# First chunk's outputs from wide products, and the first pair's sums of squares on TensorE

## The chip, the cores and the metric

The kernel runs on one core of one Trainium2 chip. The metric is the device time of one execution in microseconds (us). Before the change it is 990.29 us, the median of three runs (990.25 to 992.25). All times below that belong to a trace come from one profiled execution, which took 989.57 us.

## What is computed

Attention with random features over 4 batches, 8 heads, 576 positions, 64 values a head and 128 features, then two gated layers on its output:

```python
def phi(x):
    proj = np.einsum('bhsd,md->bhsm', x, omega)
    sq = np.sum(x * x, axis=-1, keepdims=True) / 2.0
    h = proj - sq
    h = h - np.max(h, axis=-1, keepdims=True)
    return np.exp(h) / np.sqrt(m)
q_p, k_p = (phi(q_s), phi(k_s))
kv = np.einsum('bhsm,bhsd->bhmd', k_p, v)
z = np.sum(k_p, axis=2)
num = np.einsum('bhsm,bhmd->bhsd', q_p, kv)
den = np.einsum('bhsm,bhm->bhs', q_p, z)[..., None] + 1e-06
x = num / den                                # 2304 tokens x 512
x = (silu(x @ w_gate) * (x @ w_val)) @ w_out   # 512 -> 1536 -> 512
x = (x @ w_a * (x @ w_b)) @ w_out2
```

All inputs are float32 (q_s and k_s are q and k, scaled).

## The kernel before

The 2304 tokens are cut into five chunks that end at 512, 1024, 1280, 1792 and 2304. The heads go in four pairs, two heads of 64 values to the 128 partitions. Everything that the kernel does is recorded in a plan first: each operation with its engine, an assumed cost, a due time and the tiles that it reads and writes. A list scheduler then fixes one order for each engine. `KEPT` is a tuple of seeds that shift the due times a little, so another tuple gives another order of all operations, not only of those that the diff touches. Every engine takes its list strictly in that order, and SP's list is the order of the loads.

For a pair of heads of the first batch, `keys` loads k twice, d-major (`xT`, 64 values of two heads on 128 partitions by tokens) and token-major (`kt`), and v (`vt`). `features` makes the projections (L642, into ps_m or ps_p, `bd` holds omega), the sums of squares (the token-major tile is squared by ScalarE, L579, in place, and reduced by VectorE, L583, into `s`), the biases (maximum by L653, then L656 and L660) and the exponentials on ScalarE (L666, into `kf`). TensorE sums kf with v (L702, ps_kv), ScalarE copies these sums to `kvs` (L708 the products with v, L712 the sums of the features themselves). For q of the first chunk `queries` does the same into `qf`, and `own` makes the outputs: TensorE transposes qf (L815), ScalarE copies the result to `fT` (L818), TensorE multiplies it with kvs in pieces of 128 tokens by 65 columns a head (L835), VectorE adds 1e-6 to the denominators (L852), takes the reciprocal (L856) and multiplies (L860, into `xt`), and TensorE transposes xt back to d-major (L869). `put` then splits the outputs in a high part `xh` (ScalarE, L780) and a low part `xl` (VectorE, L496) for the products of the layers in fp32r.

`layer` makes each product of a layer as a triple: xh by wh (L1011), xl by wh (L1012), xh by wl (L1013). The weights' parts come from work spread over ScalarE and VectorE: L974 and L971 on ScalarE, L977 (w64a, w64b) and L980 (w) on VectorE, then wh (ScalarE, L992) and wl (VectorE, L496). `a` (L1031, ScalarE, after a load of a table for the function) and `h` (L1039 and L1043, VectorE) are the layer's gate. At the end of the first chunk's attention nine triples with the other three pairs' xh and xl run first; then come the last pair's three, and from there on the triples follow each other. The last two chunks later go through a scheme of seven products for eight (L1080). The first 14 products (L548) multiply an identity only to keep TensorE going while inputs land.

## Time and profile before

| | |
|---|---|
| median of three runs | 990.29 us |
| the profiled execution, its own time | 989.57 us |
| its span on the core | 987.8 us |
| TensorE, products | 977.5 us busy (99%) |
| TensorE, weight loads beside them | 822.6 us (83%) |
| VectorE | 895.1 us (91%) |
| ScalarE | 714.1 us (72%) |
| GpSimd | 266.1 us (27%) |
| granted TensorE clock | full in all 40 slices |

1.8 us of the execution lie around the span. The shares are averages over the whole span; the front, in which attention is made, and the long stretch of the layers behind it have different limits, so the profile is best read by stretches of time. Busy time of TensorE counts modelled ends of overlapping products. In the rows below, a "row" of TensorE is one pass; a float32 product is two of them, a transpose one, a product of fp32r one.

### The profile page before, as it was taken

Reading aid. Unit: us, or ns where it says so; the run is one execution under the profiler, and the core shown is the slowest. Engines: PE = TensorE matmul, PEld = TensorE weight load, DVE = VectorE, ACT = ScalarE, POOL = GpSimd, SP = SyncE. Lnnn points to the kernel's source line nnn. Section 1 sums busy time; section 2 is a strip of 40 time slices with the busy share of each in tenths; the row PEclk is TensorE's granted clock in tenths of the full one; section 3 lists DMA queues with packets and bytes.
Section 4 is the critical chain, followed back from the end, with each engine's and each line's share of the span. In section 5 each row is a group of like instructions: output and inputs, shape, how many; then the busy total and the mean of one; then the engine's idle time right before and its main releaser. Section 6 shows DMA issues by size and latency. Waiting matters only on the chain. (4 is left out here: it accounts for less than half of the span.)

```text
span 987.8 us, 15428 instructions
## 1 busy us (share of the span) xinstructions
PE 977.5 (99%) x5166; PEld 822.6 (83%) x5166; DVE 895.1 (91%) x1629; ACT 714.1 (72%) x1515; POOL 266.1 (27%) x209
## 2 busy tenths in 40 slices
PE   9999999999999999999999999999999999999998
PEld 7878888888888888888789999988888888888886
DVE  6899999999978899999979989888899889989997
ACT  5987888798889997888868877676573645556351
POOL 2310023413403233364457524112020021202020
PEclk9999999999999999999999999999999999999999
DMA  8687876686876657666654465511212301121212
GB/s 279 198 272 227 242 260 188 222 241 207 270 225 199 191 175 235 207 192 218 198 188 119 141 189 164 177 57 33 74 43 64 92 26 53 33 75 44 64 33 86
DMA packets 92544, 153.12 MB, mean 155 GB/s; under 512 B 8752, under 2 KB 41392, under 8 KB 92464
## 3 DMA queue, kind: packets, MB, share of 16 engines
q1 hardware_dynamic: 92384, 152.11, 49.6%
q8 instruction: 40, 0.66, 0.3%
q14 instruction: 40, 0.33, 0.1%
q10 hardware_dynamic: 80, 0.03, 0.0%
HBM read 128.52 MB, written 23.59 MB: 154 GB/s over the span
## 5 line engine op out<-in xcount | busy, mean ns | idle before, releaser
L496 DVE TENSOR_TENSOR wl<-w,wh 128x512 fp32r<-128x512 f32 x254 | 187.3, 747 | 11.5 <-ACT wh L992 11.1
L1011 PE MATMUL ps_m<-xh,wh 128*128 128x512 f32 (+1 forms) x504 | 189.2, 375 | 1.4 <-ACT xh L780 0.7
L1012 PE MATMUL ps_m<-xl,wh 128*128 128x512 f32 (+1 forms) x504 | 184.0, 365 | 0.2 <-DVE xl L496 0.2
L1013 PE MATMUL ps_m<-xh,wl 128*128 128x512 f32 (+1 forms) x504 | 183.8, 365 | 0.0
L992 ACT ACTIVATE wh<-w 128x512 fp32r<-128x512 f32 x220 | 136.9, 633 | 34.9 <-DVE w L980 19.4
L496 POOL TENSOR_TENSOR rs<-xT,rs 64x576 fp32r<-64x576 f32 (+4 forms) x48 | 69.3, 1443 | 225.1 <-ACT rs L599 105.7
L1011 PEld LDWEIGHTS ps_m<-xh,wh 128*128 128x128 f32 x504 | 95.2, 189 | 16.3 <-issue 1.7
L1013 PEld LDWEIGHTS ps_m<-xh,wl 128*128 128x128 f32 x504 | 95.1, 189 | 15.8
L1012 PEld LDWEIGHTS ps_m<-xl,wh 128*128 128x128 f32 x504 | 95.3, 189 | 12.8 <-DVE xl L496 0.5
L1011 PE MATMUL ps_m<-hh,wh 128*128 128x512 f32 (+1 forms) x252 | 94.5, 375 | 0.0
L1012 PE MATMUL ps_m<-hl,wh 128*128 128x512 f32 (+1 forms) x252 | 92.0, 365 | 0.0
L1013 PE MATMUL ps_m<-hh,wl 128*128 128x512 f32 (+1 forms) x252 | 91.9, 365 | 0.0
L977 DVE SCALAR_TENSOR_TENSOR w64a<-w64a 128x512 uint32<-128x512 uint32 x90 | 68.3, 762 | 4.1 <-ACT w64a L974 3.7
L980 DVE SCALAR_TENSOR_TENSOR w<-w,w64a 128x512 uint32<-128x512 uint32 x90 | 65.4, 729 | 3.7 <-ACT w L971 3.6
L974 ACT ACTIVATE w64a<-w64a 128x512 uint32<-128x512 uint32 x90 | 60.9, 684 | 3.2 <-DMA w64a<-w 3.1
L971 ACT ACTIVATE w<-w64a 128x512 f32<-128x512 f32 x90 | 60.6, 677 | 0.1
L1011 PEld LDWEIGHTS ps_m<-hh,wh 128*128 128x128 f32 x252 | 47.6, 189 | 8.5 <-issue 2.0
L1013 PEld LDWEIGHTS ps_m<-hh,wl 128*128 128x128 f32 x252 | 47.6, 189 | 7.9
L1012 PEld LDWEIGHTS ps_m<-hl,wh 128*128 128x128 f32 x252 | 47.7, 189 | 6.2
L1046 ACT ACTIVATE hh<-h 128x512 fp32r<-128x512 f32 (+1 forms) x72 | 40.2, 560 | 17.0 <-DVE h L1043 15.0
L496 DVE TENSOR_TENSOR hl<-h,hh 128x512 fp32r<-128x512 f32 (+1 forms) x72 | 49.2, 685 | 0.7 <-ACT hh L1046 0.3
L900 POOL TENSOR_TENSOR xt<-qf,fT 128x512 f32<-128x512 f32 (+2 forms) x31 | 35.4, 1145 | 49.2 <-ACT qf L666 23.0
(842 smaller groups left out, 2630.5 us busy)
## 6 DMA issues: line engine op xcount, KB each, us to landing
w64a<-w SPq DMA_DIRECT2D x90, 512.0 KB, 4.2
w<-kept SPq DMA_DIRECT2D x180, 256.0 KB, 2.7
kept<-w SPq DMA_DIRECT2D x72, 256.0 KB, 4.8
w64b<-w SPq DMA_DIRECT2D x18, 512.0 KB, 4.7
kt<-k_t SPq DMA_DIRECT2D x16, 320.0 KB, 3.7
vt<-v_t SPq DMA_DIRECT2D x16, 320.0 KB, 4.3
xT<-kT SPq DMA_DIRECT2D x15, 288.0 KB, 3.9
qt<-q_t SPq DMA_DIRECT2D x16, 256.0 KB, 3.6
```

What stands on the lines that cost most here:

```text
L496: eng.tensor_tensor(out=out, in0=a, in1=hi.bitcast(F32), op=ALU.subtract)
L900: nc.gpsimd.tensor_tensor(out=pr.tile.rearrange("p (t h m) -> p t h m", t=2, h=2)[lo_:hi_, i:i + m], in0=f.tile[lo_:hi_, g + i:g + i + m], ...
L971: on(ACT, act(CW + 50), due - ahead - 10, lambda: nc.scalar.activation(out=w.tile, in_=raw.tile[:, :, 1].bitcast(F32), func=AF.Abs, scale= ...
L974: on(ACT, act(CW + 50), due - ahead - 10, lambda: nc.scalar.activation(out=raw.tile[:, :, 0], in_=raw.tile[:, :, 0], func=AF.Copy, scale=0 ...
L977: on(DVE, dve(CW, True), due - ahead - 9, lambda: nc.vector.scalar_tensor_tensor(out=raw.tile[:, :, 0], in0=raw.tile[:, :, 1], scalar=0x80 ...
L980: on(DVE, dve(CW, True), due - ahead - 9, lambda: nc.vector.scalar_tensor_tensor(out=w.tile.bitcast(U32), in0=w.tile.bitcast(U32), scalar= ...
L992: on(ACT, act(CW), due - ahead - 7, lambda: nc.scalar.activation(out=hi.tile.rearrange("p a c -> p (a c)"), in_=w.tile, func=AF.Copy), rea ...
L1011: nc.tensor.matmul(o, lhsT=hi.tile[:, wi], rhs=a, start=first, stop=False)
L1012: nc.tensor.matmul(o, lhsT=hi.tile[:, wi], rhs=b, start=False, stop=False)
L1013: nc.tensor.matmul(o, lhsT=lo.tile[:, wi], rhs=a, start=False, stop=last)
L1046: on(ACT, act(n), due + 2, lambda h=h, hh=hh: nc.scalar.activation(out=hh.tile[:, 0:n], in_=h.tile[:, 0:n], func=AF.Copy), reads=[(h,)], w ...
```

## The change

Three things change.

- `own`: for each of the four pairs the first chunk's outputs come from two calls of two products each, over all 512 tokens at once with 64 result rows a head. One call has the sums of features, repeated over 64 columns, as weights and gives the denominators for each of the 64 values; the other has kvs and gives the numerators. Both land d-major in PSUM. VectorE transposes the denominators in 32 x 32 blocks, adds 1e-6 on one value of each block's row (16 a partition), takes the reciprocal of these 16, transposes them back, repeated, and multiplies the numerators in place. The transposes back on TensorE are gone, and `put` reads the product.
- `features`, for the first pair (`SQUARES = 1`) of the first batch and chunk: the token-major tiles of k and q are not loaded. ScalarE squares the d-major tile, TensorE sums over the partitions with `head` (128 x 2, ones for the rows of a head) in products of 128 tokens by 2 columns, and VectorE copies the 10 and 8 results to `s`.
- `KEPT` holds nine other seeds, so the order of all lists changes.

```diff
     KEPT = (
-        100000, 100002, 100011, 100017, 100041, 100092, 100155, 100377, 100485, 100539,
-        100593, 100638, 100683,
+        100001, 100002, 100007, 100107, 100134, 100242, 100288, 100611, 100936,
     )
...
+    head = fixed("head", [P, 2])
...
+    r_few = ring("few", 1, [P, 2, NT // 32])
...
+    SQUARES = 1
...
+        for h in range(2):
+            for i in range(2):
+                on(DVE, dve(2), -1e6, lambda h=h, i=i: nc.vector.memset(
+                    head.tile[h * D:(h + 1) * D, i:i + 1], float(h == i)), writes=[(head, (h, i))])
...
+        if squares:
+            def of_tok():
+                return tok.tile.rearrange("p t c -> p (t c)")[:, 0:width]
+            on(ACT, act(width), due - 4, lambda: nc.scalar.activation(
+                out=of_tok(), in_=rT.tile[:, 0:width], func=AF.Square),
+                reads=[(rT, *rT.state)], writes=[(tok,)])
+            total = ps_t.buf()
+
+            def add_up():
+                for t in range(nt):
+                    nc.tensor.matmul(total.tile[:, 2 * t:2 * t + 2],
+                                     lhsT=of_tok()[:, step * t:step * t + P], rhs=head.tile,
+                                     start=True, stop=True)
+            on(PE, pe(0.16 * nt), due - 2, add_up, reads=[(tok,), (head, *head.state)],
+               writes=[(total,)])
+            on(DVE, dve(2 * nt), due - 2, lambda: nc.vector.tensor_copy(
+                s.tile[:, 0:nt].rearrange("p t h -> p (t h)"), total.tile[:, 0:2 * nt]),
+                reads=[(total,)], writes=[(s,)])
+        else:
...
-        on(SP, dma(320), due - 8, lambda: nc.sync.dma_start(out=tok.tile, in_=bass.AP(
+        squares = b == 0 and p < SQUARES
+        squares or on(SP, dma(320), due - 8, lambda: nc.sync.dma_start(out=tok.tile, in_=bass.AP(
...
-        fT, xt = r_fT.buf(), r_xt.buf()
+        kv = sums[t0 // S, p]
+        fT = r_fT.buf()
...
-                        on(PE, pe(0.233), d, lambda ps=ps, g=g, i=i, h=h, b=b, col=col:
-                           nc.tensor.matmul(
-                               ps.tile[:, col + VA * h:col + VA * (h + 1)],
-                               lhsT=fT.tile[:, h, P * (g + i):P * (g + i + 1)],
-                               rhs=sums[b, p].tile[:, h], start=True, stop=True,
-                               skip_group_check=True),
...
+        den, num, rec = ps_t.buf(), ps_t.buf(), r_ft.buf()
+
+        def times(ps, weights):
+            def run():
+                for h in range(2):
+                    nc.tensor.matmul(ps.tile[h * D:(h + 1) * D, 0:n], lhsT=weights(h),
+                                     rhs=fT.tile[:, h, 0:n], start=True, stop=True)
+            return run
+        on(PE, pe(0.52), d, times(den, lambda h: kv.tile[:, h, D:VA].to_broadcast([P, D])),
+           reads=[(kv, 1), (fT, *fT.state)], writes=[(den,)])
+        on(PE, pe(0.52), d + 0.1, times(num, lambda h: kv.tile[:, h, 0:D]),
+           reads=[(kv, 0), (fT, *fT.state)], writes=[(num,)])
+        few = r_few.buf()
+        on(DVE, dve(n), d, lambda: nc.vector.transpose(out=rec.tile[:, 0:n], in_=den.tile[:, 0:n]),
+           reads=[(den,)], writes=[(rec,)])
+        on(DVE, dve(n // 32, True), d, lambda: nc.vector.tensor_scalar(
+            out=few.tile[:, 0], in0=rec.tile.rearrange("p (b j) -> p b j", j=32)[:, :, 0],
+            scalar1=eps, scalar2=None, op0=ALU.add), reads=[(rec,)], writes=[(few,)])
+        on(DVE, dve(8 * n // 32), d, lambda: nc.vector.reciprocal(out=few.tile[:, 1], in_=few.tile[:, 0]),
+           writes=[(few,)])
+        on(DVE, dve(n), d, lambda: nc.vector.transpose(
+            out=rec.tile[:, 0:n], in_=few.tile[:, 1].unsqueeze(2).to_broadcast([P, n // 32, 32])),
+           reads=[(few,)], writes=[(rec,)])
+        on(DVE, dve(n), d, lambda: nc.vector.tensor_tensor(
+            out=num.tile[:, 0:n], in0=num.tile[:, 0:n], in1=rec.tile[:, 0:n], op=ALU.mult),
+            reads=[(rec,)], writes=[(num,)])
+        put(1, c, p, num, n, due + length)
```

Three places in the order of the engines' lists follow; a number behind a name is its buffer, and the last is its place in the program's list of tiles. In the changed kernel the projections are L667, the sums of squares L592, the products of the outputs L857, the exponentials L691, fT L847, xh L806, w64a L982, w L985, wl and xl L497, wh L997, kvs L734 and L738, the squaring L585.

TensorE at the start, before:

```order
L548 MATMUL ps_t0_66<-ident0_70 128x128 x7
L642 MATMUL ps_m0_61<-bd0_71,xT0_75 128x256 x2
L642 MATMUL ps_m1_62<-bd0_71,xT0_75 128x256 x2
L642 MATMUL ps_m2_63<-bd0_71,xT0_75 128x256
L642 MATMUL ps_p0_64<-bd0_71,xT1_76 128x256 x2
L642 MATMUL ps_p1_65<-bd0_71,xT1_76 128x256 x2
L642 MATMUL ps_m0_61<-bd0_71,xT2_77 128x256
```

and now:

```order
L554 MATMUL ps_t0_66<-ident0_70 128x128 x7
L667 MATMUL ps_p0_64<-bd0_71,xT1_76 128x256 x2
L667 MATMUL ps_p1_65<-bd0_71,xT1_76 128x256
L667 MATMUL ps_m0_61<-bd0_71,xT0_75 128x256
L592 MATMUL ps_t1_67<-head0_89,kt0_81 128x2 x5
L667 MATMUL ps_m0_61<-bd0_71,xT0_75 128x256
L592 MATMUL ps_t0_66<-head0_89,qt0_108 128x2 x4
L667 MATMUL ps_m1_62<-bd0_71,xT0_75 128x256 x2
L667 MATMUL ps_p1_65<-bd0_71,xT1_76 128x256
```

The projections of q (from xT1) come ahead of those of the keys (from xT0), and the two groups of sums of squares stand among the projections.

VectorE at the last pair's outputs, before:

```order
L852 TENSOR_SCALAR den0_99<-ps_t1_67 128x4
L856 RECIPROCAL rec0_102<-den0_99 128x4
L977 SCALAR_TENSOR_TENSOR w64a_1_161<-w64a_1_161 128x512
L860 TENSOR_TENSOR xt0_114<-ps_t1_67,rec0_102 128x256
L852 TENSOR_SCALAR den1_100<-ps_t0_66 128x4
L496 TENSOR_TENSOR wl4_179<-w320_164,wh4_172 128x512
L856 RECIPROCAL rec1_103<-den1_100 128x4
L860 TENSOR_TENSOR xt0_114<-ps_t0_66,rec1_103 128x256
L977 SCALAR_TENSOR_TENSOR w64a_2_162<-w64a_2_162 128x512
L980 SCALAR_TENSOR_TENSOR w321_165<-w321_165,w64a_1_161 128x512
L496 TENSOR_TENSOR xl3_126<-ps_t1_67,xh3_118 128x512
```

and now:

```order
L865 STREAM_TRANSPOSE ft0_113<-ps_t1_67 128x512
L982 SCALAR_TENSOR_TENSOR w64a_1_163<-w64a_1_163 128x512
L867 TENSOR_SCALAR few0_103<-ft0_113 128x16
L497 TENSOR_TENSOR wl3_180<-w323_169,wh3_173 128x512
L870 RECIPROCAL few0_103<-few0_103 128x16
L985 SCALAR_TENSOR_TENSOR w320_166<-w320_166,w64a_0_162 128x512
L872 STREAM_TRANSPOSE ft0_113<-few0_103 128x512
L985 SCALAR_TENSOR_TENSOR w321_167<-w321_167,w64a_1_163 128x512
L875 TENSOR_TENSOR ps_t0_66<-ps_t0_66,ft0_113 128x512
L497 TENSOR_TENSOR wl4_181<-w320_166,wh4_174 128x512
L982 SCALAR_TENSOR_TENSOR w64a_2_164<-w64a_2_164 128x512
L497 TENSOR_TENSOR xl3_128<-ps_t0_66,xh3_120 128x512
```

The steps between the products and xl are five, three of them 512 wide, where they were six on half the columns or on four values; the weight work of `layer` stands among them in both.

ScalarE ahead of the last pair's sums of keys, before:

```order
L780 ACTIVATE xh2_117<-ps_t0_66 128x512
L666 ACTIVATE qf1_108<-ps_p0_64,bias2_95 128x128 x4
L666 ACTIVATE qf1_108<-ps_p1_65,bias0_93 128x128 x4
L818 ACTIVATE fT0_109<-ps_t1_67 128x2x256
L666 ACTIVATE kf0_82<-ps_m2_63,bias5_98 128x128 x2
L818 ACTIVATE fT0_109<-ps_t0_66 128x2x256
L992 ACTIVATE wh2_170<-w322_166 128x512
L992 ACTIVATE wh3_171<-w323_167 128x512
L708 ACTIVATE kvs0_87<-ps_kv0_68 128x2x64
L712 ACTIVATE kvs0_87<-ps_kv0_68 128x2
```

and now:

```order
L691 ACTIVATE qf1_110<-ps_p0_64,bias3_97 128x128 x4
L997 ACTIVATE wh1_171<-w321_167 128x512
L847 ACTIVATE fT0_111<-ps_t0_66 128x2x256
L806 ACTIVATE xh2_119<-ps_t1_67 128x512
L691 ACTIVATE qf1_110<-ps_p1_65,bias4_98 128x128 x4
L691 ACTIVATE kf0_82<-ps_m2_63,bias5_99 128x128 x2
L979 ACTIVATE w64a_0_162<-w64a_0_162 128x512
L847 ACTIVATE fT0_111<-ps_t0_66 128x2x256
L997 ACTIVATE wh2_172<-w322_168 128x512
L734 ACTIVATE kvs0_87<-ps_kv0_68 128x2x64
L738 ACTIVATE kvs0_87<-ps_kv0_68 128x2
```

The third pair's xh has moved behind the first four exponentials of the last pair's q, a weight copy and one fT.

## Rows read from the trace of the kernel before

**Rows 1.** Windows: start:end, length, busy us (instructions) by engine, granted clock, DMA share, GB/s

```profile
0.00:10.00 10.00, 8.63 (x32) 7.30 (x32) 4.16 (x15) 3.10 (x6) 1.77 (x10) 1.00 0.77 237
10.00:20.00 10.00, 9.23 (x70) 8.70 (x70) 6.40 (x20) 6.91 (x26) 2.71 (x3) 1.00 0.83 284
20.00:30.00 10.00, 9.26 (x57) 7.31 (x55) 9.05 (x26) 8.04 (x27) 3.15 (x3) 1.00 0.75 252
30.00:40.00 10.00, 9.45 (x71) 8.70 (x71) 7.12 (x27) 9.18 (x27) 2.71 (x6) 1.00 0.73 237
40.00:50.00 10.00, 9.68 (x63) 7.92 (x61) 9.93 (x23) 9.47 (x29) 4.16 (x2) 1.00 0.62 193
...
60.00:987.80 927.80, 922.68 (x4844) 776.33 (x4842) 849.18 (x1503) 669.38 (x1393) 251.57 (x187) 1.00 0.48 149
```

**Rows 2.** TensorE's waits from 60 us: waiting line <- releaser, total, times, longest

```profile
PE ps_kv L1011 <- DVE h L1039: 1.0, 2, 0.8
PE ps_m L1011 <- DVE a L1036: 0.2, 1, 0.2
```

**Rows 3.** TensorE's timeline at the last pair: start, us, instructions, idle before

```profile
49.15 2.00 PE L835 MATMUL ps_t<-kvs,fT 128*128 128x65 f32 x16 [0.32 <-ACT kvs L712]
...
54.57 0.50 PE L1011 MATMUL ps_m<-xh,wh 128*128 128x512 f32 x1 [0.69 <-ACT xh L780]
55.30 0.50 PE L1012 MATMUL ps_m<-xl,wh 128*128 128x512 f32 x1 [0.22 <-DVE xl L496]
...
58.13 0.50 PE L1011 MATMUL ps_m<-xh,wh 128*128 128x512 f32 x1 [0.50 <-ACT a L1031]
```

**Rows 4.** ScalarE's timeline there

```profile
48.86 0.23 ACT L712 ACTIVATE kvs<-ps_kv 128x2 f32<-128x2 f32 x1
...
53.92 0.60 ACT L780 ACTIVATE xh<-ps_t 128x512 fp32r<-128x512 f32 x1 [1.15 <-PE ps_t L869]
...
57.48 1.09 ACT L1031 ACTIVATE a<-ps_m 128x512 f32<-128x512 f32 x2
```

**Rows 5.** VectorE's timeline there

```profile
53.31 0.68 DVE L977 SCALAR_TENSOR_TENSOR w64a<-w64a 128x512 uint32<-128x512 uint32 x1
53.91 0.68 DVE L980 SCALAR_TENSOR_TENSOR w<-w,w64a 128x512 uint32<-128x512 uint32 x1
54.55 0.69 DVE L496 TENSOR_TENSOR xl<-ps_t,xh 128x512 fp32r<-128x512 f32 x1
```

**Rows 6.** VectorE's groups by form, 0 to 60 us: busy us, mean ns, idle before

```profile
L583 DVE TENSOR_REDUCE s<-kt 128x10 f32<-128x640 f32 x5 | 4.1, 810 | 0.0
L860 DVE TENSOR_TENSOR xt<-ps_t,rec 128x256 f32<-128x256 f32 x8 | 3.4, 421 | 0.1
...
L583 DVE TENSOR_REDUCE s<-qt 128x8 f32<-128x512 f32 x4 | 2.7, 680 | 0.4 <-ACT qt L579 0.4
...
L856 DVE RECIPROCAL rec<-den 128x4 f32<-128x4 f32 x8 | 1.4, 174 | 0.1
...
L852 DVE TENSOR_SCALAR den<-ps_t 128x4 f32<-128x4 f32 x8 | 1.3, 157 | 0.8 <-PE ps_t L835 0.7
```

**Rows 7.** TensorE's groups by form, 0 to 60 us

```profile
L835 PE MATMUL ps_t<-kvs,fT 128*128 128x65 f32 x64 | 7.9, 274 | 0.3 <-ACT kvs L712 0.3
...
L869 PE MATMUL ps_t<-ident,xt 128*128 128x128 f32 x16 | 3.1, 276 | 0.0
```

**Rows 8.** TensorE's timeline at the second chunk's outputs

```profile
550.93 1.08 PE L944 MATMUL ps_t<-ft,kvs 128*64 128x512 f32 x4
551.94 0.38 PE L616 MATMUL ps_p<-oms,rs 128*128 128x256 f32 x1
```

**Rows 9.** TensorE's and ScalarE's timelines at the start

```profile
4.51 3.71 PE L642 MATMUL ps_m<-bd,xT 128*128 128x256 f32 x10
8.07 1.99 PE L642 MATMUL ps_p<-bd,xT 128*128 128x256 f32 x8
...
9.12 0.63 ACT L666 ACTIVATE kf<-ps_m,bias 112x128 f32<-112x128 f32 x2 [2.79 <-DVE bias L656]
```

More of the change, by code (lines that the diff above doesn't have):

```diff
@@ L562, in constants, with features @@
                     reads=[(x,)], writes=[(oms, (i, h))], after=ALONE)
-    def features(rT, tok, nt, step, f, due, length, how, psum, first, rows=None):
+    def features(rT, tok, nt, step, f, due, length, how, psum, first, squares, rows=None):
         width = step * (nt - 1) + P
@@ L574, in features, with square @@
         s = r_s.buf()
-        def square():
-            x = tok.tile[:, 0:nt].rearrange("p t c -> p (t c)")
-            if first:
-                nc.scalar.activation(out=x, in_=x, func=AF.Square)
-            else:
-                nc.gpsimd.tensor_tensor(out=x, in0=x, in1=x, op=ALU.mult)
-        on(*((ACT, act(nt * P)) if first else (POOL, pool(nt * P, True))), due - 4, square, writes=[(tok,)])
-        on(DVE, dve(nt * P), due - 2, lambda: nc.vector.tensor_reduce(
-            out=s.tile[:, 0:nt], in_=tok.tile[:, 0:nt].rearrange("p t (h d) -> p t h d", h=2),
-            op=ALU.add, axis=AX.X), reads=[(tok,)], writes=[(s,)])
+        if squares:
[16 more added lines that the diff above has]
+        else:
+            def square():
+                x = tok.tile[:, 0:nt].rearrange("p t c -> p (t c)")
+                if first:
+                    nc.scalar.activation(out=x, in_=x, func=AF.Square)
+                else:
+                    nc.gpsimd.tensor_tensor(out=x, in0=x, in1=x, op=ALU.mult)
+            on(*((ACT, act(nt * P)) if first else (POOL, pool(nt * P, True))), due - 4, square, writes=[(tok,)])
+            on(DVE, dve(nt * P), due - 2, lambda: nc.vector.tensor_reduce(
+                out=s.tile[:, 0:nt], in_=tok.tile[:, 0:nt].rearrange("p t (h d) -> p t h d", h=2),
+                op=ALU.add, axis=AX.X), reads=[(tok,)], writes=[(s,)])
         stacks = []
@@ L693, in keys @@
         features(rT, tok, KT, TS, f, due, length, how, ps_m if how == WHOLE else ps_p,
-                 first=due < 4, rows=rows)
+                 first=due < 4, squares=squares, rows=rows)
         out = r_kvs.buf()
@@ L795, in queries @@
                for b in range(t0 // S, (t1 - 1) // S + 1)])
-        on(SP, dma(n / 2), due - 8, lambda: nc.sync.dma_start(
+        squares = c == 0 and p < SQUARES
+        squares or on(SP, dma(n / 2), due - 8, lambda: nc.sync.dma_start(
             out=tok.tile[:, 0:nt], in_=bass.AP(q.tensor, q.offset + t0 * DM + p * P,
@@ L800, in queries @@
         f = r_qf.buf()
-        features(rT, tok, nt, P, f, due, length * 0.5, how, ps_p, first=due < 8)
+        features(rT, tok, nt, P, f, due, length * 0.5, how, ps_p, due < 8, squares)
         (shared if how == STACKED or c == 1 else own)(c, p, f, due, length)
@@ L866, in own @@
-        ps = ps_t.buf()
-        for t in range(nt):
-            parts = [key for key in xt.state if key[0] == t]
-            on(PE, pe(0.11), due + length, lambda t=t: nc.tensor.transpose(
-                ps.tile[:, P * t:P * (t + 1)], xt.tile[:, P * t:P * (t + 1)],
-                ident.tile), reads=[(xt, *parts), (ident,)], writes=[(ps, t)])
-        ps.state[None] = [[w for t in range(nt) for w in ps.state[t][0]], []]
-        put(1, c, p, ps, n, due + length)
+        d = due + length * 0.8
```

37 lines of the change are left out of this document (removed).

## The prediction

> **What bounds the kernel now.** I read the table of windows first, then TensorE's waits, then the timelines of the three busy engines at the last of the four head pairs. From 60 us to the end TensorE is busy for 922.68 of 927.8 us [rows 1], and all that it waits for there on other engines is 1.2 us [rows 2]. So that long stretch cannot be shortened by anything but fewer products, and the change takes none out of it. What is left is the front, 0 to 60 us, where the first chunk's attention is made before the long products can run. There VectorE has slack in the middle (from 10 to 40 us it is busy 6.40 + 9.05 + 7.12 = 22.57 of 30 us, so 7.4 us are free) and none at the end (9.93 of 10 us from 40 to 50) [rows 1]. The dense stretch begins when the last pair is through: its sums of keys are copied at 48.86 + 0.23 = 49.09 us [rows 4], the products of the outputs start at 49.15, and TensorE then waits 0.69 us for xh, 0.22 for xl and 0.50 for a, the last of these ending at 58.13 us [rows 3]. After 58.13 us it hardly stops. Hence the time moves by as much as this point moves.
>
> The profiled execution took 989.57 us, 0.72 under the median of 990.29. I make the sum as a shift and add it to either.
>
> **Part 1, TensorE's side of the new outputs.** Removed for each pair: sixteen rows of 65 columns (2.00 us at 49.15 us [rows 3]; 7.9 us for all 64 [rows 7]) and four transposes back (3.1 us for 16, so 0.78 a pair at most [rows 7]). Added: two products over 512 columns for both heads. The trace has no such product in this place; the nearest is the second chunk's, 64 result rows by 512 columns, both heads, four rows in 1.08 us, the next work starting 1.01 us after it began [rows 8]. Two of these are 2.0 us. So TensorE gains at most 0.8 us a pair; the last pair's transposes stood on the path, the rest beside ScalarE's and VectorE's work.
>
> **Part 2, VectorE's side.** Removed for each pair: two each of L860 (0.42), L856 (0.17) and L852 (0.16), 1.5 us [rows 6]. Added: a transpose of 512 columns, an addition on 16, a reciprocal on 16, a transpose back and a multiplication of 512. None of the transposes is in the trace. The lower bound is the pitch of other 512-wide instructions, 53.91 − 53.31 = 0.60 us; the upper is their 0.68 us without overlap [rows 5]. I take 0.68 for work (a reading from PSUM does not hurry it), 0.16 and 0.17 for the two narrow ones as in the old ones of 4 values: 3 × 0.68 + 0.33 = 2.4 us, 0.9 more for each pair.
>
> **Part 3, the last pair's chain.** Before, xh of the last pair starts at 53.92 us [rows 4], 4.83 after the sums of keys. In the new order these follow the copy of the sums: the first product, 1.08 + 0.05; then, on VectorE in order, transpose, w64a, addition, wl, reciprocal, w, transpose back, w, multiplication (by what they write). Four of the nine are weight work put between (w64a, wl and twice w); all of them count, since VectorE takes them in order. With 0.60 for seven wide ones, 0.1 and 0.18 for the narrow, and 0.09 more for the end of the last: 4.57. Then 0.05 to ScalarE: 5.75, which is 0.9 later than 4.83. If VectorE may begin when the next work in [rows 8] does, 1.01 instead of 1.08, it is 0.85. With 0.68 each, no overlap and 0.16 and 0.17 for the narrow: 1.13 + 5.09 + 0.05 = 6.27, 1.4 later. I take **+1.2**, a little above the middle for the weight work that itself waits for ScalarE (wl waits for wh). Two weight instructions stand between the multiplication and xl, which puts xl some 0.6 later against xh than before (54.55 − 53.92 = 0.63 [rows 4, 5]); that costs nothing, because TensorE next stops for a in any case, which starts at 57.48, is there some 0.6 later [rows 4] and hangs on xh by ScalarE's queue: in both orders three 512-wide instructions and one table load lie between xh and a. TensorE has five product triples between the new products and the first that wants xh, where it had three between the old ones and that; they fill the wait and do not lengthen it (fifteen rows; a row of the dense stretch takes 922.68 / 4844 = 0.19 us on average [rows 1], so some 3 us of the 5.75).
>
> **Part 4, the first pair's sums of squares.** Removed: two loads, 320 + 256 KB. At the 284 GB/s of 10 to 20 us [rows 1] all later inputs come 576 / 284 = 2.0 us earlier. Also removed are two reductions, 0.81 + 0.68 [rows 6]. Added: eighteen rows with two result columns on TensorE, two copies of 10 and 8 values on VectorE (0.16 each), four small fills at the start where VectorE has nothing to do. ScalarE squares 576 + 512 columns instead of 640 + 512: nothing. The nine products of the sums are eighteen rows; for one of them I take what a row of 65 columns costs, 7.9 / 64 = 0.123 us [rows 7], 2.2 us in all. On the way to the first exponential TensorE now has ten projection rows (three of q's projections are first, then the two of the first keys, five of two rows each) and ten rows of sums: 4.51 + 3.71 [rows 9] + 10 × 0.123 = 9.45 us. A wide reduction at 0.68 [rows 6] and two short steps of 0.16 on VectorE, priced as L852, make 10.45, where the first exponential now starts at 9.12 us [rows 9]: 1.4 later (with the signals between). With rows of two columns at nothing it is 0.2 later; that is the other end.
>
> The Trainium skill, TensorEngine Tiling (Array Packing), Instruction Overhead, says that a product costs some 60 cycles however few its columns, one column as much as sixty. As an estimate from that page the ten rows would take 10 × 60 / 2400 = 0.25 us instead of 1.23, and with half of that 1.0 off the forecast it would be 991.6. The trace's rows with 65 columns take 0.123 us, and no row with two columns is in it.
>
> **Part 5, when the last pair's sums are ready.** Work on VectorE ahead of that point: three earlier pairs × 0.9 = +2.7, sums of squares −1.5 + 0.3, so +1.5 net. Low end: the inputs' 2.0 us arrive in full and only the 1.5 counts, −0.5. High end: VectorE full throughout and the start's delay unhidden, +1.5 + 1.4 = +2.9. The 7.4 us free from 10 to 40 take the start's delay and some of the work; the full stretch after 40 us does not. I take **+0.6**, nearer the low end for that room.
>
> **Sum.** +0.6 + 1.2 = **+1.8 us**: 991.4 us on the profiled execution's 989.57, 992.1 on the median. Its own range: −0.5 + 0.85 = +0.35 to +2.9 + 1.4 = +4.3, so 990.6 to 994.6. The order of everything else changes with the seeds; what that can give back behind 60 us is the 1.2 us of [rows 2], and it may cost as much, which I leave beside the sum.
>
> **Rivals.** *Faster:* inputs 2.0 us earlier and a new order that puts VectorE's work into its free 7.4 us. If half of these are filled, the last sums of keys come 3.7 us earlier, and with the chain's +1.2 that is −2.5: 987.8 us. For it: VectorE idles for 3.6 us from 10 to 20 us [rows 1], and the two loads come out ahead of that. Against: the first pair itself starts later. It holds if VectorE's idle time from 10 to 40 us falls below 4 us.
>
> *No change:* 1.2 of the 2.0 us arrive, and pay for the chain: 990.3. For it: a chunk's later pairs have all their inputs by then. Against: VectorE's added 1.5 us in the full stretch.
>
> *Slower, ScalarE's order:* ScalarE has the third pair's xh ahead of the last pair's second four exponentials of q, the last two of k, fT and the sums of keys. That xh now waits for the multiplication at the end of the VectorE chain (4.57 us by part 3), where before it waited for short steps (0.16 + 0.17 + 0.42 [rows 6] and two transposes of 3.1 / 16 = 0.19 [rows 7], 1.1 in all). If VectorE is behind there, everything in ScalarE's queue waits: 4.6 − 1.1 = 3.5 on the last sums, +1.2 of the chain: +4.7, 995.0 us. It decides from 2 us of idle time ahead of that xh on. Against: the new order puts four exponentials, a weight copy and fT ahead of it, which fill some 3 us.
>
> *Slower, TensorE's pace at the start:* the first ten projection rows after the warming take 3.71 us, 0.37 each, the next eight 1.99, 0.25 each, at a granted clock of 1.00, the 2.4 GHz level, for the whole window [rows 1, 9]. If small rows among the projections keep the slow pace going, the next eight projection rows cost 8 × 0.12 = 1.0 more and the eighteen rows of sums twice their 2.2: +3.2 on the first pair's exponentials, of which VectorE's free time may hide half. That is +1.8 + 1.6 = +3.4, 993.7 us. The Trainium skill, TensorE: Matmul & The Clock Gate, Part 1, says that the engine's default is the throttled clock and that activity releases it; the trace's 1.00 does not show the low level, while its slow first rows would fit.
>
> **How the numbers follow.** Forecast 0.50, faster 0.15, no change 0.18, ScalarE's order 0.12, TensorE's pace 0.05. A measurement tells about 0.2% of this kernel, 1.98 us, from no change. The forecast's range lies about half on either side of +1.98: 0.25 same, 0.25 slower. Same: 0.18 + 0.25 = 0.43; slower: 0.25 + 0.12 + 0.05 = 0.42; faster 0.15. The range from 987.7 to 995.1 leaves out about half of the faster and of the slowest case, 0.07 + 0.08.
>
> **What would show it.** In the profile of the changed kernel: the new pair of products 1.0 us each; the wide VectorE transposes 0.6 to 0.7; the rows of two columns 0.12; the first exponential at 10.5; the last sums of keys at 49.7; xh 6.0 after them; the a that opens the dense stretch at 59.9 us; TensorE's waits after it still 1 to 2 us. Wrong would make it: a transpose of far over 0.7, a stall in ScalarE ahead of the third xh, or waits behind 60 us.

## The result, and the profile after

The changed kernel takes 999.01 us (998.80 to 999.55, four runs) against 990.77 us for the kernel before beside it: 1.0088 times as long, with a 95% interval of 1.0076 to 1.0100. That is 8.2 us slower. The forecast was 1.8 us, its range ended at 995.1. The traced execution took 998.82 us, with a span of 996.8. Three runs far off all others of the same kernel (1213.47 and 3470.70 us of the kernel before, 1090.79 us of the kernel that has only the changed due times) are left out of the numbers below.

First, the table of windows of the changed kernel, which answers to [rows 1]; columns as there (start:end, length, busy us of TensorE, its weight loads, VectorE, ScalarE, GpSimd, granted clock, share of the DMA engines, GB/s).

```profile
10.00:20.00 10.00, 8.06 (x40) 6.67 (x40) 7.33 (x23) 5.07 (x18) 3.54 (x3) 0.84 0.86 256
...
70.00:996.80 926.80, 918.67 (x4820) 771.89 (x4818) 841.04 (x1496) 664.15 (x1382) 244.54 (x186) 1.00 0.49 148
```

The last row runs from 70 us to the end: TensorE is idle for 926.80 − 918.67 = 8.1 us of it, where before it was 5.1 in the whole stretch from 60 us [rows 1]. So part of the loss is not in the front. The second row has a granted clock of 0.84. These are TensorE's waits from 120 us on (waiting line <- releaser: total, times, longest), as in [rows 2]:

```profile
PE ps_m L1018 <- DVE wl L497: 2.5, 2, 1.3
PE ps_kv L1016 <- DVE a L1041: 1.0, 2, 0.6
PE ps_m L1016 <- DVE a L1041: 0.7, 1, 0.7
```

4.2 us against 1.2. Next, the last pair of the first chunk, TensorE and then ScalarE with the start of the kernel (start, length, what, idle before), which answer to [rows 3, 4, 9]:

```profile
52.84 1.94 PE L857 MATMUL ps_t<-fT,kvs 128*64 128x512 f32 x8
...
59.14 0.49 PE L1016 MATMUL ps_m<-xh,wh 128*128 128x512 f32 x1 [0.69 <-ACT xh L806]
60.30 0.50 PE L1017 MATMUL ps_m<-xl,wh 128*128 128x512 f32 x1 [0.66 <-DVE xl L497]
...
62.73 0.50 PE L1016 MATMUL ps_m<-xh,wh 128*128 128x512 f32 x1
```

```profile
10.50 1.14 ACT L691 ACTIVATE kf<-ps_m,bias 112x128 f32<-112x128 f32 x4 [3.32 <-DVE bias L685]
14.47 1.14 ACT L691 ACTIVATE kf<-ps_m,bias 112x128 f32<-112x128 f32 x4 [2.83 <-DVE bias L681]
...
48.39 0.60 ACT L806 ACTIVATE xh<-ps_t 128x512 fp32r<-128x512 f32 x1 [0.42 <-DVE ps_t L875]
...
52.08 0.24 ACT L738 ACTIVATE kvs<-ps_kv 128x2 f32<-128x2 f32 x1
...
58.49 0.60 ACT L806 ACTIVATE xh<-ps_t 128x512 fp32r<-128x512 f32 x1
```

The long stretch opens at 62.73 us where it opened at 58.13. Of these 4.6 us, 3.2 are there when the sums of keys are copied (52.32 against 49.09) and 1.3 come by the chain to xh (6.17 us against 4.83). From there to TensorE's last row it is 930.3 us (62.73 to 993.08), before 925.7 (58.13 to 983.85): another 4.6. The waits make 3.0 of these (4.2 − 1.2); the other 1.6 stand in no wait that the profile lists and were not traced further.

The chain itself on VectorE, where [rows 5] had the old one:

```profile
53.97 0.72 DVE L865 STREAM_TRANSPOSE ft<-ps_t 128x512 f32<-128x512 f32 x1
54.61 0.65 DVE L982 SCALAR_TENSOR_TENSOR w64a<-w64a 128x512 uint32<-128x512 uint32 x1
55.18 0.17 DVE L867 TENSOR_SCALAR few<-ft 128x16 f32<-128x16 f32 x1
55.26 0.69 DVE L497 TENSOR_TENSOR wl<-w,wh 128x512 fp32r<-128x512 f32 x1
55.86 0.25 DVE L870 RECIPROCAL few<-few 128x16 f32<-128x16 f32 x1
56.03 0.63 DVE L985 SCALAR_TENSOR_TENSOR w<-w,w64a 128x512 uint32<-128x512 uint32 x1
56.57 0.70 DVE L872 STREAM_TRANSPOSE ft<-few 128x512 f32<-128x512 f32 x1
57.19 0.65 DVE L985 SCALAR_TENSOR_TENSOR w<-w,w64a 128x512 uint32<-128x512 uint32 x1
57.76 0.69 DVE L875 TENSOR_TENSOR ps_t<-ps_t,ft 128x512 f32<-128x512 f32 x1
```

The five new steps take 0.72, 0.17, 0.25, 0.70 and 0.69 us, and between each two of them stands one weight instruction of some 0.6 us.

At the start, TensorE's rows of the sums of squares and its first long pause; what VectorE and GpSimd do ahead of the second four exponentials; and the granted clock after TensorE's pause (windows of TensorE: start:end, length, busy, clock, DMA share, GB/s):

```profile
7.42 1.17 PE L592 MATMUL ps_t<-head,kt 128*128 128x2 f32 x10
8.45 0.68 PE L667 MATMUL ps_m<-bd,xT 128*128 128x256 f32 x2
8.97 0.95 PE L592 MATMUL ps_t<-head,qt 128*128 128x2 f32 x8
...
15.66 0.70 PE L667 MATMUL ps_m<-bd,xT 128*128 128x256 f32 x2 [1.94 <-ACT kf L691]
```

```profile
11.53 0.68 DVE L678 TENSOR_REDUCE bias<-ps_p 128x4 f32<-128x512 f32 x1
12.13 1.03 DVE L681 SCALAR_TENSOR_TENSOR bias<-s,bias 128x4 f32<-128x4 f32 x1
...
13.42 0.68 DVE L678 TENSOR_REDUCE bias<-ps_p 128x4 f32<-128x512 f32 x1
```

```profile
11.89 1.25 POOL L606 TENSOR_TENSOR kt<-kt 128x640 f32<-128x640 f32 x1 [9.47 <-PE ps_m L667]
```

```profile
16.00:18.00 2.00, 2.00 (x13) 0.71 0.76 239
18.00:20.00 2.00, 2.00 (x8) 0.50 0.87 280
```

Ten rows of two columns take 1.17 us, eight 0.95. The first four exponentials start at 10.50 us, as forecast, but the second four at 14.47, where before the last eight of ten ran from 10.15 on:

```profile
10.15 2.18 ACT L666 ACTIVATE kf<-ps_m,bias 112x128 f32<-112x128 f32 x8
```

TensorE, which waits for them, stands for 1.94 us, and from about 17 to 20 us it has the lower of its two levels, 1.2 GHz instead of 2.4.

### The profile page after: what moved, and what is told of

Read it like the earlier page. It is cut to its first block, busy times and chain, and to the rows that moved or that the text cites. A ratio compares the mean times of both kernels' runs of the same rounds, so it can differ in the third digit from the quotient of the medians.

```text
span 996.8 us, 15354 instructions
## 1 busy us (share of the span) xinstructions
PE 981.6 (98%) x5136; PEld 818.9 (82%) x5136; DVE 895.4 (90%) x1629; ACT 715.1 (72%) x1515; POOL 260.0 (26%) x209
## 4 chain that ended last, share of the span: by engine, by line
PE 79%; DVE 10%; ACT 6%; DMA 2%; issue 2%; POOL 1%; SPq 0%; POOLq 0%; ACTq 0%; DVEq 0%
PE ps_m L1085 13%; PE ps_m L1016 11%; PE ps_m L1018 11%; PE ps_m L1017 11%; PE ps_t L1085 9%; PE ps_p L1085 8%; PE ps_kv L1085 4%; DVE wl L497 2%; DMA w64a<-w 2%; PE ps_p L641 2%; DVE w L985 2%; DVE w64a L982 1%; PE ps_p L667 1%; PE ps_t L949 1%; PE ps_kv L728 1%
## 5 line engine op out<-in xcount | busy, mean ns | idle before, releaser
L497 DVE TENSOR_TENSOR wl<-w,wh 128x512 fp32r<-128x512 f32 x254 | 193.5, 770 | 14.6 <-ACT wh L997 14.0
L997 ACT ACTIVATE wh<-w 128x512 fp32r<-128x512 f32 x220 | 137.0, 631 | 42.6 <-DVE w L985 18.9
L497 POOL TENSOR_TENSOR rs<-xT,rs 64x576 fp32r<-64x576 f32 (+4 forms) x48 | 68.1, 1420 | 252.8 <-ACT rs L624 114.4
L1016 PE MATMUL ps_m<-hh,wh 128*128 128x512 f32 (+1 forms) x240 | 90.6, 378 | 0.0
L1017 PE MATMUL ps_m<-hl,wh 128*128 128x512 f32 (+1 forms) x240 | 88.6, 369 | 0.0
L1018 PE MATMUL ps_m<-hh,wl 128*128 128x512 f32 (+1 forms) x240 | 88.6, 369 | 0.0
L985 DVE SCALAR_TENSOR_TENSOR w<-w,w64a 128x512 uint32<-128x512 uint32 x90 | 67.1, 747 | 1.6 <-ACT w L976 1.2
L982 DVE SCALAR_TENSOR_TENSOR w64a<-w64a 128x512 uint32<-128x512 uint32 x90 | 65.5, 735 | 1.6 <-ACT w64a L979 1.5
L1018 PEld LDWEIGHTS ps_m<-hh,wl 128*128 128x128 f32 x240 | 45.3, 189 | 7.9
L1016 PEld LDWEIGHTS ps_m<-hh,wh 128*128 128x128 f32 x240 | 45.4, 189 | 7.7 <-issue 1.3
L1017 PEld LDWEIGHTS ps_m<-hl,wh 128*128 128x128 f32 x240 | 45.4, 189 | 6.2
L497 DVE TENSOR_TENSOR hl<-h,hh 128x512 fp32r<-128x512 f32 (+1 forms) x72 | 44.6, 624 | 2.9 <-ACT hh L1051 2.9
```

Source lines behind the costliest of these rows:

```text
L497: eng.tensor_tensor(out=out, in0=a, in1=hi.bitcast(F32), op=ALU.subtract)
L982: on(DVE, dve(CW, True), due - ahead - 9, lambda: nc.vector.scalar_tensor_tensor(out=raw.tile[:, :, 0], in0=raw.tile[:, :, 1], scalar=0x80 ...
L985: on(DVE, dve(CW, True), due - ahead - 9, lambda: nc.vector.scalar_tensor_tensor(out=w.tile.bitcast(U32), in0=w.tile.bitcast(U32), scalar= ...
L997: on(ACT, act(CW), due - ahead - 7, lambda: nc.scalar.activation(out=hi.tile.rearrange("p a c -> p (a c)"), in_=w.tile, func=AF.Copy), rea ...
L1016: nc.tensor.matmul(o, lhsT=hi.tile[:, wi], rhs=a, start=first, stop=False)
L1017: nc.tensor.matmul(o, lhsT=hi.tile[:, wi], rhs=b, start=False, stop=False)
```

## The experiments

Two theories were set against each other. **A:** the order of everything else, which the other seeds change, costs the time. **B:** the new operations do, in whatever order. All runs were made beside the kernel before (medians of 990.25 to 990.58 us); the numbers in brackets behind a ratio are its 95% interval.

**1. Seeds and operations apart.** The shifts of the due times are drawn for each operation in turn, so each kernel here was made to draw them as the other does for the operations that both have; operations of one alone are not shifted.

```diff
+    def ghosts(self, n):
+        self.draws += [None] * n
...
-            for o in self.ops:
+            for o in self.draws:
```

All new operations, due times of before:

> The changed kernel's operations, with every operation that both kernels have given the due time that the kernel before gives it (same seeds, same draws). Theory A, the order that the new seeds make costs the 8.2 us: 990 to 994 us. Theory B, the new operations cost it whatever the order: 997 to 1000 us, and the last pair's sums of keys again near 52.3 us (49.1 before).

Measured: 1000.89 us, ratio 1.0116 (1.0079 to 1.0152).

The wide outputs alone (`SQUARES = 0`):

> Only the wide outputs of the first chunk, token-major sums of squares as before, due times of before. Theory A: 991 to 993, by the longer chain of the last pair alone (+1.3 us, as the changed kernel's trace has it). Theory B with the wide outputs as the cause: 996 or more.

Measured: 1004.15 us, 1.0142 (1.0110 to 1.0175).

The sums of squares alone (`own` of before):

> Only the first pair's sums of squares on TensorE, outputs as before, due times of before. Theory A: 989 to 992. Theory B with the sums of squares as the cause (first pair's exponentials late by 1.4 and then by 4.3 us as in the changed kernel): 994 or more.

Measured: 994.77 us, 1.0051 (1.0028 to 1.0073).

The old operations, due times of the changed kernel:

> The kernel before with the due times of the changed kernel for all operations that both have. Theory A: 996 to 1000 us, with stalls of TensorE behind 200 us like those of the changed kernel (3 to 4 us). Theory B: 990 to 992.

Measured: 1009.11 us, the median of three runs (1008.56 to 1012.16), 1.0198 (1.0176 to 1.0220).

Neither theory as written holds: the first three come out as B expects, the fourth as A, and beyond A's range. The fourth kernel has no new operation and loses some 19 us; so the seeds can cost more than the whole change. But the first has the old due times and is as slow as the changed kernel. The reason, read from the scheduler's code, is that due times do not fix an order: it takes what is ready, and with other operations in the front other things are ready from there on. Neither tuple of seeds served the other kernel's operations. An order had to be held, not a set of seeds.

**2. The order held.** In the next kernels each operation's due time is its place in the order of one of the two kernels; the scheduler then follows that order nearly everywhere that the operations are the same (its rule that puts off a change of function table is switched off).

```diff
     def shift(self):
-        for k in self.KEPT:
...
+        for o, due in zip(self.ops, DUES):
+            if due is not None:
+                o.due = due / 1000
...
-                if table and other and o.due > t - 6.0:
+                if table and other and o.due > t + 1e6:
```

Old and new were crossed at the point where the long stretch opens. New operations and order up to there, old order behind:

> The changed kernel's operations; up to the point where the dense stretch begins every engine has the changed kernel's order, behind it the order of the kernel before (TensorE's list behind that point differs from it in 5 of 1352 operations). Theory A, half of the loss is the order of the rear: about 995 us (990.6 + the front's 4.6), TensorE idle behind the front about 1 us as in the kernel before. Theory B, the rear's loss follows from the later front or the new operations: 998 to 1000 us, idle there 4 us.

Measured: 993.16 us (992.26 to 996.09), 1.0038 (1.0022 to 1.0053), so +2.9 us. That is under theory A's 995. In its traced run, the slowest of the five, TensorE waits for 1.1 us behind the front (h 0.6, wl 0.3, a 0.2), and the long stretch lasts 925.9 us (64.66 to 990.53), both as before: all that this run loses, it loses in the front.

The old operations and order up to there, the new order behind:

> The kernel before with its own order up to the start of the dense stretch and the changed kernel's order behind it, no new operation in it. Theory A: about 995 us, TensorE idle 4 us behind the front. Theory B: 990 to 992 us.

Measured: 994.76 us, 1.0049 (1.0034 to 1.0064), so +4.5 us without one new operation. In its trace the long stretch opens at 59.00 us, 0.9 later than before though the order up to there is the old one, and lasts 929.3 us (to 988.30), 3.6 more than before. Its waits from 60 us on:

```profile
PE ps_m L1451 <- DVE wl L934: 1.7, 2, 1.2
PE ps_kv L1449 <- DVE a L1474: 0.8, 2, 0.4
PE ps_m L1449 <- DVE a L1474: 0.7, 1, 0.7
```

They are the same ones as in the changed kernel: wl, then a. +2.9 and +4.5 make 7.4 of the 8.2 us. Theory A is right for the rear. The trace of the changed kernel shows what happens at the longest of these waits; VectorE and GpSimd, and then TensorE's next row:

```profile
234.45 1.26 DVE L916 TENSOR_SCALAR den<-den 128x4 f32<-128x4 f32 x1
235.62 0.68 DVE L497 TENSOR_TENSOR hl<-h,hh 128x512 fp32r<-128x512 f32 x1
236.22 0.17 DVE L919 RECIPROCAL rec<-den 128x4 f32<-128x4 f32 x1
236.31 0.65 DVE L912 TENSOR_REDUCE den<-xt 128x4 f32<-128x512 f32 x1
236.88 0.68 DVE L678 TENSOR_REDUCE bias<-ps_p 128x4 f32<-128x512 f32 x1
237.48 0.15 DVE L916 TENSOR_SCALAR den<-den 128x4 f32<-128x4 f32 x1
237.55 0.68 DVE L497 TENSOR_TENSOR wl<-w,wh 128x512 fp32r<-128x512 f32 x1
```

```profile
234.07 1.61 POOL L905 TENSOR_TENSOR xt<-qf,fT 128x512 f32<-128x512 f32 x1 [0.86 <-ACT w L976]
```

```profile
238.28 0.50 PE L1018 MATMUL ps_m<-xh,wl 128*128 128x512 f32 x1 [1.32 <-DVE wl L497]
```

From 234.45 us on six instructions stand ahead of wl, five of them the second chunk's attention (den, rec and the reduction into bias), one 1.26 us long. The same step takes 0.15 us at 237.48; the long one ends at 235.71, 0.03 us after the product that GpSimd had begun before it (234.07 to 235.68). At 12.13 us it was the same: 1.03 us instead of 0.15, to 13.16, beside GpSimd's squaring from 11.89 to 13.14. So an order also sets what VectorE meets on GpSimd, which the scheduler's costs foresee only as far as its times hold. TensorE has wl's product next in its list and waits 1.32 us. VectorE is busy for nine tenths of the long stretch [rows 1], so there is little room between wl and its due moment; which work stands ahead of it and beside it is set by the order.

**3. The new operations in the old order.** Each new operation stands at the place of the one that it replaces.

> All the new operations, put into the order of the kernel before at the places of those that they replace, the rest in the old order. If the prediction's price of the new operations was right and only the order of everything else was not: 991 to 993.5 us. If the new operations cost the front's 4.6 us in any order: 995 or more.

Measured: 993.46 us, 1.0036 (1.0022 to 1.0051): +3.2 us. The price of the operations was 1.8 in the prediction, with its own range to 4.3. With their new order the same front cost 2.9 (experiment 2), so the new order of the front adds nothing that these runs can tell, and the account is: some 3 us for the operations, in the front, and some 4.5 for the new order of the rear. In the trace of this kernel the long stretch opens at 62.35 us and lasts 925.8 (to 988.11), as before. Of the 4.2 us by which it opens later, 2.0 are there when the sums of keys are copied (51.11 against 49.09), and 1.9 come from there to xh (6.7 us against 4.8). Most of the first part shows at the second pair's q, whose exponentials wait for VectorE and start 1.9 us later than before; here, and then before:

```profile
25.87 1.14 ACT L1126 ACTIVATE qf<-ps_p,bias 128x128 f32<-128x128 f32 x4 [2.03 <-DVE bias L1120]
```

```profile
23.98 1.14 ACT L666 ACTIVATE qf<-ps_p,bias 128x128 f32<-128x128 f32 x4 [1.11 <-DVE bias L660]
```

> Only the wide outputs, in the old order at the old places; sums of squares and loads as before. By the chain alone (+1.3 us as measured in the changed kernel): 991 to 993. If the sums of squares make up for part of it in the front: later than the kernel with both. If the wide outputs are nearly free: 990 to 991, and then the sums of squares carry what the kernel with both shows.

Measured: 995.91 us, 1.0055 (1.0040 to 1.0070): the wide outputs alone have the slower median than both parts together, with intervals that overlap.

> Only the first pair's sums of squares on TensorE and its two token-major loads gone, in the old order, outputs as before. By part 4 of the prediction (first exponential 0.2 to 1.4 us later, inputs 2.0 us earlier): 989.5 to 991.5. If the sums of squares are what helps in the kernel with both against the one with the wide outputs alone (993.5 against 995.9): 988 to 989.5.

Measured: 990.19 us, 0.9999 (0.9990 to 1.0009). The sums of squares are free in this order. The ten exponentials of the keys run from 8.90 us there. In the five traces with the small rows in the old order they start at 8.5 to 9.4 us, in the three without them at 9.0 to 9.1; the spread follows the pace of TensorE's first rows, which differs from trace to trace. In the changed kernel, where q's projections come ahead of the keys', they start at 10.50. So the prediction's 1.4 us of delay go with the new order of the first rows and not with the eighteen small ones alone. The +3.2 us are thus put down to the wide outputs. That these show 5.7 without the other part is not explained: the granted clock is a likely part of it (0.995 to 0.998 in the four runs, and in the trace at half for three stretches, from 25.1, 45.6 and 62.6 us on, where the kernel with both parts has one), the inputs' earlier arrival with the sums of squares another; neither is shown.

**4. What the wide outputs cost.** In the kernel with all new operations in the old order, TensorE's rows at the last pair, and the granted clock just after:

```profile
58.47 0.50 PE L1451 MATMUL ps_m<-xh,wh 128*128 128x512 f32 x1 [2.80 <-ACT xh L1241]
...
61.13 0.63 PE L1452 MATMUL ps_m<-xl,wh 128*128 128x512 f32 x1
...
62.35 0.80 PE L1451 MATMUL ps_m<-xh,wh 128*128 128x512 f32 x1 [0.17 <-ACT a L1471]
```

```profile
61.00:62.00 1.00, 1.00 (x3) 0.50 0.95 359
...
63.00:64.00 1.00, 1.00 (x5) 0.72 0.73 166
```

TensorE stands for 2.80 us for xh; from 60.1 to 63.5 us the granted clock is 0.50, and the row at 61.13 takes 0.63 instead of 0.39 us. In this trace that costs little: slow as its rows are, TensorE still waits 0.17 us for a at 62.35, and a hangs on xh by ScalarE's list. Only the four rows from 62.35 to 63.70 are late by the clock, some 0.3 us (an estimate: 1.35 us here, 1.04 for the same four from 62.73 in the changed kernel). Two remedies for the pause were tried. Work in it:

```diff
+        if p == 3:
+            spare = ps_p.buf()
+            def keep_busy():
+                for _ in range(11):
+                    nc.tensor.matmul(spare.tile[:, 0:P], lhsT=ident.tile, rhs=ident.tile,
+                                     start=True, stop=True)
+            on(PE, pe(2.4), 56.0, keep_busy, reads=[(kv, 0, 1), (num,), (ident,)], writes=[(spare,)])
```

> The kernel with all new operations in the old order, plus eleven products with an identity whose result nobody reads (2.4 us of TensorE work), put where TensorE waits 2.8 us for the last pair's xh. If the pause costs more than itself, because the granted clock is at half from 60.1 to 63.5 us after it: 1 to 2 us faster than without them, 991.5 to 992.5, and no half clock there. If the clock has nothing to do with the pause: the same 993.5 or up to 0.5 more.

Measured: 996.9 us, 1.0068 (1.0051 to 1.0085): 3.4 slower. Its clock by windows:

```profile
20.00:30.00 10.00, 7.75 (x38) 0.83 0.75 249
...
60.00:70.00 10.00, 8.67 (x37) 1.00 0.73 223
```

The clock behind the pause was held, as meant. But TensorE, quicker there, only waits longer for a, 1.1 us instead of 0.17: a starts 4.2 us after xh by ScalarE's list (63.37 and 59.20), where it was 3.9. The lower clock came in this run at an earlier pause, of 1.80 us, between 20 and 30 us; in the kernel without the extra products that pause was 2.15 us long and left the clock alone. The long stretch, too, is 1.3 us longer (64.02 to 991.06), its order having changed along with the rest. So this run does not price the clock.

The chain in one piece, its weight work behind it:

```diff
+            def chain():
+                nc.vector.transpose(out=rec.tile[:, 0:n], in_=den.tile[:, 0:n])
...
+            on(DVE, dve(3 * n), d, chain, reads=[(den,)], writes=[(rec,), (few,), (num,)])
```

> All new operations in the old order, with the last pair's five VectorE steps in one piece, the weight work behind them instead of between. If part 3 of the prediction is right that every interleaved instruction counts (four of 0.6 us): xh 2 us earlier than in the kernel in the old order (57.8 there), TensorE's pause of 2.8 us mostly gone, 990.5 to 992. If wl then comes late and takes the place of the wait: 993 to 994.

Measured: 992.12 us over ten runs (989.83 to 993.95), 1.0015 (1.0005 to 1.0024). TensorE's two rows there:

```profile
55.81 0.49 PE L1465 MATMUL ps_m<-xh,wh 128*128 128x512 f32 x1 [1.23 <-ACT xh L1241]
56.91 0.50 PE L1466 MATMUL ps_m<-xl,wh 128*128 128x512 f32 x1 [0.61 <-DVE xl L932]
```

The time is just above the 990.5 to 992 expected, and its interval touches that of the kernel with the chain in pieces (1.0022 to 1.0051). xh comes 55.16 − 50.24 = 4.9 us after the sums of keys, where it was 6.7, and TensorE waits 1.2 + 0.6 us instead of 2.8 + 0.2. The four of the ten runs with a mean granted clock of 1.000 took 989.83 to 991.18 us, the six below it (0.997 to 0.999) 991.70 to 993.95. With the chain in one piece and no half clock the new operations are as fast as the old to within some 0.3 us; that rests on four runs picked by their clock.

For all four pairs:

> All new operations in the old order, the five VectorE steps in one piece for all four pairs. If the earlier pairs' chains also delay ScalarE's list: 988.5 to 990.5, ahead of the kernel with the last chain alone in one piece (992.1). If only the last chain counts: 991 to 993.

Measured: 994.38 us, 1.0041 (1.0028 to 1.0054), slower than with the last alone; every one of its five runs had a clock of 0.995 to 0.998. In its trace TensorE waits 1.0 us for xh and 1.9 for xl, and the granted clock is at half from 57.1 to 63.9 us. Whether the earlier chains themselves do better in pieces, or only the clock makes the difference, was not followed further.

In the changed kernel's own order, the last chain in one piece:

> The changed kernel in its own order, with the last pair's five VectorE steps in one piece and its four weight instructions behind them. If they stand on the path as part 3 says: xh 1.8 us earlier (58.5 there), 997 to 997.8 us against 999.0. If wl3 behind the chain becomes late: 998.5 to 999.5.

Measured: 998.06 us, 1.0076 (1.0063 to 1.0090), a median 0.9 under the changed kernel's, half of what was expected and with intervals that overlap. xh is there 4.5 us after the sums of keys instead of 6.2, but xl is not:

```profile
59.01 0.50 PE L1466 MATMUL ps_m<-xl,wh 128*128 128x512 f32 x1 [2.36 <-DVE xl L932]
```

TensorE has xh early and then waits 2.36 us for xl, because six weight instructions stand between the chain and xl; from 59.8 to 63.2 us the granted clock is then at half. The wait changed its name.

**5. Is there a better order?** A search over due times by the kernel's own assumed costs, equally long for both sets of operations (the wide products at 1.0 us and the sums at 0.23 us a product as traced).

> The kernel before with another order of the same operations, from a search over due times (nothing new computed). If the order alone is worth as much as the whole change: 985 to 988. If the old order is already as good as such a search gives on the chip: 989.5 to 992.

Measured: 995.12 us, 1.0046 (1.0031 to 1.0061).

> All new operations with an order from the same search as long, with the wide products at 1.0 us and the sums of squares at 0.23 us a product as traced. If the order was the changed kernel's whole fault: as fast as or faster than the searched old operations. If the new operations cost 1 to 3 us whatever the order: behind it by that, 988 to 992.

Measured: 993.14 us, 1.0028 (1.0019 to 1.0038). Neither beats the kernel before. The clock is not why: all thirteen runs had a mean granted clock of 0.999 or 1.000. The search goes by assumed costs, and where they mislead it was not followed. Between the two, the new operations are not the slower ones.

New operations in the front with the clock held at its pauses without moving anything else were not tried, nor an order searched by measured times.

## Why the prediction was wrong

**The step that failed** is the sentence behind the sum: that the order of everything else could give back the 1.2 us of [rows 2] "and it may cost as much". It cost 4.5 us (old front, new rear), 3.6 of them behind the front by the trace. The working took the old trace's waits behind 60 us as a measure of both sides. For a gain they are one: no more than 1.2 us could be won. For a loss they say nothing, since another order can put any work of VectorE ahead of what TensorE wants next, and with VectorE busy for 91% there was little room to make up for it. That the seeds had changed stood in the diff and in its description; rows of the lists behind 60 us were not compared.

**Part 5** is the term of the sum that was too small. It gave +0.6 for the last sums of keys; the trace of the changed kernel shows +3.2, outside its own high end of 2.9, and the one with all new operations in the old order +2.0. Its low end rested on all later inputs coming 2.0 us earlier. With the sums alone in the old order, SP issues the second pair's v at 4.22 us instead of 5.08, but the third pair's v at 14.02 as before, so that gain does not last beyond the second pair. The first exponential came out right (10.50 for 10.5) by two misses that cancel: the rows ahead of it ended at 9.13 us, forecast 9.45, and VectorE's steps behind them took 1.4, forecast 1.0. It was also the only one that was priced. The second four came 4.3 us later than before, by VectorE's list, in which two reductions of q's products stand ahead of the step on the keys' second bias and one step is held up beside GpSimd; and TensorE lost its clock over the pause that this made. That these make the +3.2 is argued, not shown: in the old order, without them, +2.0 are there. Measured across runs the new front costs 2.9 us, with a spread from 992.26 to 996.09; the spread goes with the clock (0.999 at the fast end, 0.994 at the slow one), as the windows of the slowest show:

```profile
10.00:20.00 10.00, 9.57 (x49) 0.83 0.76 227
...
50.00:60.00 10.00, 10.00 (x37) 0.77 0.50 176
```

**Part 3** was right: xh 6.17 us after the sums of keys, forecast 6.0 (5.75 to 6.3 by its bounds), two products 1.94 us, forecast 2.0; wide steps of VectorE 0.69 to 0.72, forecast 0.6 to 0.7. In one piece the chain takes 4.9 us. It was also right that the later xl costs nothing: TensorE waits 0.66 us for it, but the stretch opens 4.24 us after xh (62.73 − 58.49), before 4.21. What it left out does not show in the changed kernel, where five triples fill the wait: in the old order three do, the pause is 2.8 us, and rows at half clock follow.

**Part 4**: 0.117 us for a row of two columns, forecast 0.123, so the nearest row was the right one. The Trainium skill's 60 cycles (TensorEngine Tiling (Array Packing), Instruction Overhead), 0.025 us as an estimate, are not what the trace shows for these rows. The delay of 1.4 us went with the order, by the run with the sums alone.

**The rivals.** TensorE's pace came true in kind, not at the place given: at 17 us, after a pause, not over the first rows. ScalarE's list ahead of the third xh stood for 0.42 us, far from the 2 us from which it would have decided. Of the prediction's own signs of being wrong one came: waits behind 60 us. The faster case wanted VectorE's idle time from 10 to 40 us under 4 us; it was 6.0 (7.33 + 7.03 + 9.60 us busy of 30). The Trainium skill, TensorE: Matmul & The Clock Gate, Part 1, has the throttled clock as the default that activity releases; the windows at 0.50 behind the pauses agree with it.

## What to carry to other kernels

Where a change touches what sets the order of a whole program, price that first: compare the lists where the old trace has no waits, and take the old waits as the bound of a gain, never of a loss. To tell an operation's price from its order's, hold the old order and put the new operation at the old place; here that turned +8.2 us into 0.0 for one part and +3.2 for the two together. And a chain of short steps on an engine that also does background work costs what stands between its steps; moving that work behind the chain helps only as long as nothing needed next stands behind it (here xl).

## What was not expected of the hardware

After a pause of 1.94 us, in the changed kernel, TensorE had a granted clock of 0.71 and 0.50 in the windows of 16 to 20 us, after one of 2.80 us 0.50 to 0.72 from 60 to 64 us. It is not the same each time: a wait of 2.1 us near 24 us left the clock at 1.00 in the kernel with all new operations in the old order, and one of 1.8 us at the same place was followed by 0.83 over the ten us around it in the kernel with the extra products. The kernel with the last chain in one piece spreads by 4 us with it (989.83 to 993.95); the kernel before, at 0.999 to 1.000 in all its runs, spreads by 3 (989.25 to 992.25).

The first rows of a run are not alike either: rows of 256 columns start 0.427 us apart until 5 to 7.5 us and then 0.216 in most traces, and 0.216 apart from the first on in a few; in one, that of the sums of squares alone with the old due times, it took until 18 us, and that run was 999.65 us, where four of its six were 992.96 to 995.19. 0.427 is twice 0.216, as 2.4 GHz is twice 1.2, though the profile gives a granted clock of 1.00 there; so the 1.00 of the first window, in the kernel before too [rows 1, 9], does not tell TensorE's pace.

A short step of VectorE can take as long as the instruction that GpSimd has begun before it: 1.26 us at 234.45 and 1.03 us at 12.13 for steps of 0.15, each ending 0.02 to 0.03 us after GpSimd's.
